# Linear attention and a gated feed-forward on one core: numerators in two column halves in plain float32, normalizers in four column strips

## The chip, the core and the metric

The kernel runs on one core of a Trainium2 chip. Of the core's engines, TensorE (PE in the profile, its weight loads PEld) multiplies matrices into PSUM, VectorE (DVE) and ScalarE (ACT) work element by element, and SyncE (SP) issues the transfers between the chip's memory and SBUF. GpSimd (POOL) does almost nothing here. The metric is the device time in microseconds (us) of one execution; less is better. A head is an attention head; "pair" below means two heads of one batch entry, which the kernel treats together.

## The reference, cut to what matters

```python
# q, k, v: 8 batches x 8 heads x 576 positions x 64; w_phi: 64 x 128
def phi(x):
    proj = einsum('bhsd,df->bhsf', x, w_phi)                     # 128 features
    proj = proj - max(abs(proj), axis=-1, keepdims=True)
    return concatenate([exp(proj), exp(-proj)], axis=-1)         # 256 features
q_p, k_p = phi(q), phi(k)
kv = einsum('bhsf,bhsd->bhfd', k_p, v)                           # 256 x 64 per head
z = sum(k_p, axis=2)                                             # 256 per head
num = einsum('bhsf,bhfd->bhsd', q_p, kv)
den = einsum('bhsf,bhf->bhs', q_p, z)[..., None] + 1e-06
attn = num / den
# x: 4608 tokens x 512; w_gate, w_val: 512 x 1536; w_out: 1536 x 512
out = (1 / (1 + exp(-(x @ w_gate))) * (x @ w_val)) @ w_out
```

`num` is called the numerator and `den` the normalizer below. The two signs of the exponential are two products that accumulate into the same result.

## The kernel before, in words

**Attention.** Positions lie along the free dimension and features along the 128 partitions. For each of the 32 pairs `att_k` projects K (`pk`), takes the maximum of the absolute values, exponentiates (`ek`) and multiplies with V (`kvp`, line 358). V carries a column of ones, so the product has 65 rows: 64 of `kv` and one of `z`. Four small transposes (line 367, `tp`) bring it to 128 features x 65 for each head and sign. `att_q` projects Q (`pq`, lines 397 and 403), and DVE subtracts the maximum, which leaves `d` (line 428, whose instruction is kept in `marks`).

`att_num` runs once for each half of the 576 positions. ACT exponentiates `d` for both signs (`eq`, line 439). For each head the products of line 456 go into one accumulator `nm` of 65 rows: 64 rows of numerators and, as the 65th, the normalizers. ACT copies it to `ex` (line 460). `ps_n` holds a single such accumulator.

**Two number formats.** TensorE multiplies plain float32, or float32r, a float32 rounded to fewer bits, of which the trace writes fp32r on the engines that produce it. From pair 8 on (`WHOLE` = 8) the kernel splits each operand into a rounded part and a residual, and adds three float32r products in place of one float32 product: line 446 rounds the exponentials (`eqh`, ACT), line 447 takes the residual (`eql`, DVE), and `kvh` and `kvl` are the same for the key-value sums. The first eight pairs use plain float32, with `kv` unsplit.

**Normalizing.** `att_norm` gathers the 65th row of `ex` over DMA into 128 partitions x 9 (`dn`, line 469), DVE adds 1e-06 and takes the reciprocal, and two DMAs write it to memory and spread it over 64 partitions (`rb`, lines 472 and 473). `att_scale` multiplies (`xp`, line 484, once for each head) and writes x to memory (`xs`, line 491). Both run for pair i-1 while pair i is worked on.

**Feed-forward.** Five of its 12 blocks of 128 hidden features (`JA` = 5) run beside the attention, in chunks of 256 tokens, as soon as a batch entry's x is there: `gv` (line 136), then the gate on ACT and DVE, then `acc` (line 143). The other seven run after the attention, in chunks of 512 tokens (`g`, `v`, `acc`).

**What sets the order.** The program's order for a pair is: loads, `att_k`, `att_q` of the next pair, `att_norm` of the pair before, the two halves of `att_num`, `att_scale` of the pair before, and one step of loading weights. Between them `fill()` hands out units of feed-forward work. A planner then orders each engine's instructions ahead of time by priority and estimated readiness; attention work has the higher priority (`PRIORITY`), and `issue_after` ties an instruction behind another on its engine. `att_scale` is tied behind the last residual of line 447, or, where there is none, behind the subtraction of line 428. All DMAs are issued by SP in one order. PSUM has eight accumulators of 2 KB a partition: two for `gv`, three for the projections (`ps_p`, tag `pp`), one for `kvp` and `tp`, one for `nm`, one for `acc`.

Of the kernel before, what the change touches and what calls it, by code (L numbers as in the profile page):

```python
# [30 lines left out]
HS = S // 2  # L31
KVW = D + 1

JA = 5  # feed-forward blocks that run beside the attention
JR = 8  # blocks JA to JR - 1 take the attention's bytes, the others phase 1's
WHOLE = 8  # first pairs: plain float32 products, no splits
DIRECT = 4  # first pairs: K's exponentials straight from PSUM
PRIORITY = 400
RATE, LAG = 0.7, 2  # feed-forward units per slot; slots from x to its first unit


@with_exitstack
def attention_moe(
# [20 lines left out]
        for m in marks:  # L64
            stack.enter_context(tc.issue_after(m.ins))

# [1 line left out]
    weights = {}  # L68

    ebias = const.tile([P, 1], F32, name="ebias")  # L70
    vec.memset(ebias, -896.0 * 2.0**23)

    def from_f64(h, l, raw, mid, sp, nb, name):
        # h: the value cut to 12 bits; l: the other bits as an integer times their unit
        words = raw.rearrange("p (n two) -> p n two", two=2)
        lo, hi = words[:, :, 0], words[:, :, 1]
        top = sp.tile([P, DM], U32, tag="wtop", name="wtop" + name, bufs=nb)
        vec.tensor_scalar(top, hi, 0x7FFFFE00, None, op0=ALU.bitwise_and)
        relu = act.activation(top, top, AF.Relu, bias=ebias, scale=8.0)
        vec.scalar_tensor_tensor(  # L80
            top, hi, 0x80000000, top, op0=ALU.bitwise_and, op1=ALU.bitwise_or
        )
        vec.tensor_copy(h, top.bitcast(F32))
        if mid is None:
            rest, unit = hi, lo
            vec.tensor_scalar(
                hi, hi, 16, 0x01FF0000, op0=ALU.logical_shift_left, op1=ALU.bitwise_and
            )
            vec.scalar_tensor_tensor(
                hi, lo, 16, hi, op0=ALU.logical_shift_right, op1=ALU.bitwise_or  # L90
            )
        else:
            words = mid.rearrange("p (n two) -> p n two", two=2)
            rest, unit = words[:, :, 0], words[:, :, 1]
            vec.tensor_scalar(rest, rest, 0x01FFFFFF, None, op0=ALU.bitwise_and)
        vec.tensor_scalar(unit, top, 0xFF800000, None, op0=ALU.bitwise_and)
        return relu, vec.scalar_tensor_tensor(
            l, rest, 2.0**-36, unit.bitcast(F32), op0=ALU.mult, op1=ALU.mult
        )

    def load_weights(j, m, wp, sp, nb, twice):
        if m == 0:
            wh = wp.tile([P, 3 * DM], F32R, tag=f"wh{j}", name=f"wh{j}")
            wl = wp.tile([P, 3 * DM], F32R, tag=f"wl{j}", name=f"wl{j}")
            weights[j] = (wh, wl)
        wh, wl = weights[j]
        ms = slice(m * DM, m * DM + DM)
        raw = sp.tile([P, 2 * DM], U32, tag="wraw", name=f"wraw{j}_{m}", bufs=nb + 1)
        load, mid = nc.sync.dma_start(raw, w_moe[j, :, m, :].bitcast(U32)), None
        if twice:  # L110
            # the same rows two bytes on: a word then holds the bits below h's
            mid = sp.tile([P, 2 * DM], U32, tag="wmid", name=f"wmid{j}_{m}", bufs=nb)
            nc.sync.dma_start(
                mid[:, : 2 * DM - 1].bitcast(U16),
                w_moe[j, :, m, :].bitcast(U16)[:, 1 : 4 * DM - 1],
            )
        return load, *from_f64(wh[:, ms], wl[:, ms], raw, mid, sp, nb, f"{j}_{m}")
# [135 lines left out]
            xs = nxt  # L253
        out_step(*late)

# [1 line left out]
    with ExitStack() as actx:  # L257
        wp1 = actx.enter_context(tc.tile_pool(name="wp1", bufs=1))
        moe = actx.enter_context(tc.tile_pool(name="moe1", bufs=2))
        at1 = actx.enter_context(tc.tile_pool(name="at1", bufs=1, side="right"))  # L260
        at = actx.enter_context(tc.tile_pool(name="at", bufs=2, side="right"))
        ps_gv = actx.enter_context(tc.tile_pool(name="ps_gv", bufs=2, space=PSUM))
        ps_p = actx.enter_context(tc.tile_pool(name="ps_p", bufs=3, space=PSUM))
        ps_kv = actx.enter_context(tc.tile_pool(name="ps_kv", bufs=1, space=PSUM))
        ps_n = actx.enter_context(tc.tile_pool(name="ps_n", bufs=1, space=PSUM))
        ps_acc = actx.enter_context(tc.tile_pool(name="ps_o", bufs=1, space=PSUM))

        ident = at1.tile([KVW, KVW], F32, name="ident")
# [24 lines left out]
        def att_k(b, p):  # L293
# [71 lines left out]
            tp = ps_kv.tile([P, 4, KVW], F32, tag="kvp", name="tp" + n)  # L365
            for i in range(4):
                nc.tensor.transpose(tp[:, i, :], kvt[:, i, :], ident)
            if b * NP + p < WHOLE:
                kv = at.tile([P, 4, KVW], F32, tag="kv", name="kv" + n)
                act.copy(kv, tp)  # L370
                kvs[b, p] = (kv,)
            else:
                kvh = at.tile([P, 4, KVW], F32R, tag="kv", name="kvh" + n)
                kvl = at.tile([P, 4, KVW], F32R, tag="kvl", name="kvl" + n)
                split(kvh, kvl, tp)
                kvs[b, p] = (kvh, kvl)

        def att_q(b, p):
            n = f"{b}_{p}"
# [46 lines left out]
                pm.unsqueeze(2).broadcast_to([P, nj, 32]),  # L426
            )
            marks.append(vec.tensor_tensor(d, d, mb, op=ALU.subtract))
            ex = at.tile([KVW, 2, S], F32, tag="ex", name="ex" + n)
            qst[b, p] = (d, ex)  # L430

        def att_num(b, p, hf):
            n = f"{b}_{p}_{hf}"
            d, ex = qst[b, p]
            cs = slice(hf * HS, hf * HS + HS)
            terms = []
            for sg in range(2):
                e = at.tile([P, 2, HS], F32, tag="eq", name=f"eq{n}_{sg}", bufs=2)
                act.activation(e, d[:, :, cs], AF.Exp, scale=1.0 - 2.0 * sg)
                if len(kvs[b, p]) == 1:  # L440
                    terms.append([(kvs[b, p][0], e)])
                else:
                    kvh, kvl = kvs[b, p]
                    eh = at.tile([P, 2, HS], F32R, tag="eqh", name=f"eqh{n}_{sg}", bufs=2)
                    el = at.tile([P, 2, HS], F32R, tag="eql", name=f"eql{n}_{sg}", bufs=2)
                    act.copy(eh, e)
                    late[b, p, hf, sg] = vec.tensor_tensor(
                        el, e, eh.bitcast(F32), op=ALU.subtract
                    )
                    terms.append([(kvh, eh), (kvl, eh), (kvh, el)])  # L450
            for hd in range(2):
                nm = ps_n.tile([KVW, HS], F32, tag="nm", name=f"nm{n}_{hd}")
                last = len(terms[0]) - 1
                for sg in range(2):
                    for i, (a, x) in enumerate(terms[sg]):
                        nc.tensor.matmul(  # L456
                            nm, a[:, 2 * hd + sg, :], x[:, hd, :],
                            start=sg == 0 and i == 0, stop=sg == 1 and i == last,
                        )
                act.copy(ex[:, hd, cs], nm)  # L460

        def att_norm(b, p):
            n = f"{b}_{p}"
            _, ex = qst.pop((b, p))
            dn = at.tile([P, 9], F32, tag="dn", name="dn" + n)
            rb = at.tile([D, 2, S], F32, tag="rb", name="rb" + n, bufs=1)
            scr = dens[b * NP + p]
            for hd in range(2):
                nc.sync.dma_start(dn[hd * D : hd * D + D, :], ex[D : D + 1, hd, :])
            vec.tensor_scalar(dn, dn, 1e-6, None, op0=ALU.add)  # L470
            vec.reciprocal(dn, dn)
            nc.sync.dma_start(scr.rearrange("h (r c) -> (h r) c", c=9), dn)
            nc.sync.dma_start(
                rb.rearrange("p h s -> p (h s)"),
                scr.rearrange("h s -> (h s)").unsqueeze(0).broadcast_to([D, 2 * S]),
            )
            rbs[b, p] = (ex, rb)

        def att_scale(b, p):
            n = f"{b}_{p}"  # L480
            ex, rb = rbs.pop((b, p))
            xp = at.tile([P, S], F32, tag="xp", name="xp" + n, bufs=2)
            for hd in range(2):
                vec.tensor_tensor(
                    xp[hd * D : hd * D + D, :], ex[0:D, hd, :], rb[:, hd, :], op=ALU.mult
                )
            t = 0
            while t < S:
                c, o = divmod(b * S + t, CH)
                w = min(CH - o, S - t)  # L490
                nc.sync.dma_start(
                    xscr[c][:, p * CH + o : p * CH + o + w], xp[:, t : t + w]
                )
                t += w
# [31 lines left out]
        for i, (b, p) in enumerate(steps):  # L526
# [9 lines left out]
            if i:  # L536
                attend(att_norm, *steps[i - 1])
            fill()
            attend(att_num, b, p, 0)
            fill()  # L540
            attend(att_num, b, p, 1)
            if i:
                m = late.get((b, p, 1, 1), marks[-1])
                with tc.issue_after(m.ins):
                    attend(att_scale, *steps[i - 1])
            while wdone < min(3 * JA, 4 * i + 1):
                with tc.issue_after(marks[-1].ins):
# [90 lines left out]
```

## Time and profile before

| | |
|---|---|
| Median of the runs | 1304.68 us (1303.23 to 1305.15, 3 runs) |
| Profiled execution, first to last instruction | 1307.2 us |
| Mean granted TensorE clock | 0.992 |
| TensorE busy | 1269.8 us, 97% |
| VectorE busy | 877.5 us, 67% |
| ScalarE busy | 650.7 us, 50% |
| Numerators of line 456, first to last start | 23.8 to 686.7 us |

The span is that of one profiled execution, and its length is taken as this execution's own time; it lies 2.5 us above the median. Engine rows in a timeline give start and length in microseconds, engine, line, operation, the tile written and the tiles read, and partitions x elements. A group row gives a line's instructions together: how many, busy time, mean nanoseconds of one, then the idle time of the engine just before them and what ended it. "128*65" after a product means 128 rows and 65 columns of the array in use. A busy TensorE can hold overlapping products, so starts say more than lengths.

### The profile page before, as it was taken

To read this page: it belongs to the slowest core of one execution; us is meant where nothing else is said; L and a number is where in the kernel's file an instruction comes from. 1 tells how busy PE (TensorE), PEld (TensorE's weight loads), DVE (VectorE), ACT (ScalarE), POOL (GpSimd) and SP (SyncE) were. 2 spreads that over 40 slices of the span, in tenths; PEclk is the share of its full clock that TensorE was granted. 3 is DMA by queue.
4 is the path that set the end of the run, shared out by engine and by line. 5 is a ranking of instruction groups with operands and counts; after the bars stand their busy time and mean duration, and the time that the engine had idled before them with its cause. 6 is when DMAs were issued, how large, how long until landed. Compare 5 with 4: busy or idle time off the path is not lost.

```text
span 1307.2 us, 19107 instructions
## 1 busy us (share of the span) xinstructions
PE 1269.8 (97%) x7112; PEld 1070.8 (82%) x7112; DVE 877.5 (67%) x1778; ACT 650.7 (50%) x1416; POOL 0.6 (0%) x6
## 2 busy tenths in 40 slices
PE   7878999999999999999999999999999999999998
PEld 4545788999898989898998988888888888888886
DVE  5777989899899888989866958834343443434333
ACT  5754777777777787777754523322222222222221
POOL 0000000000000000000000000000000000000000
PEclk9988999999999999999999999999999999999999
DMA  5576543233233323332225424313021211202010
GB/s 190 165 216 195 167 131 100 85 107 105 86 115 86 107 84 118 94 108 76 61 69 180 130 78 132 97 65 97 1 97 33 65 50 48 97 1 97 1 65 33
DMA packets 75166, 125.12 MB, mean 96 GB/s; under 512 B 18496, under 2 KB 38080, under 8 KB 75072
## 3 DMA queue, kind: packets, MB, share of 16 engines
q1 hardware_dynamic: 75072, 123.89, 30.7%
q8 instruction: 56, 0.92, 0.3%
q14 instruction: 38, 0.31, 0.1%
HBM read 95.25 MB, written 28.46 MB: 95 GB/s over the span
## 4 chain that ended last, share of the span: by engine, by line
PE 88%; DVE 4%; DMA 4%; ACT 2%; issue 1%; SPq 0%; DVEq 0%; ACTq 0%
PE acc L143 22%; PE gv L136 17%; PE g L136 13%; PE v L136 13%; PE kvp L358 9%; PE nm L456 7%; PE pk L316 3%; PE pq L403 2%; PE pq L397 1%; DMA xs<-xp 1%; DMA q<-q 1%; DMA rb<-den 1%; DMA dn<-ex 1%; ACT ek L338 1%; DMA wraw<-w_moe 1%
## 5 line engine op out<-in xcount | busy, mean ns | idle before, releaser
L136 PE MATMUL gv<-xh,wh 128*128 128x256 f32 x720 | 208.3, 290 | 3.6 <-DVE t L156 3.4
L136 PE MATMUL gv<-xh,wl 128*128 128x256 f32 x720 | 206.5, 287 | 0.0
L136 PE MATMUL gv<-xl,wh 128*128 128x256 f32 x720 | 206.2, 286 | 0.0
L60 ACT CAST hh<-u 128x256 fp32r<-128x256 f32 (+1 forms) x153 | 75.4, 494 | 245.3 <-DVE u L157 245.1
L143 PE MATMUL acc<-wh,hh 128*128 128x512 f32 x432 | 171.3, 397 | 0.7 <-ACT y L187 0.7
L143 PE MATMUL acc<-wl,hh 128*128 128x512 f32 x432 | 169.9, 393 | 0.0
L143 PE MATMUL acc<-wh,hl 128*128 128x512 f32 x432 | 166.1, 394 | 0.1
L358 PE MATMUL kvp<-ek,v 128*65 128x256 f32 x640 | 158.6, 383 | 6.9 <-ACT ek L338 5.3
L155 DVE TENSOR_SCALAR t<-t 128x256 uint32<-128x256 uint32 (+1 forms) x153 | 52.5, 344 | 154.6 <-ACT t L152 153.7
L136 PEld LDWEIGHTS gv<-xh,wh 128*128 128x128 f32 x720 | 137.1, 191 | 10.0 <-DVE t L156 4.7
L136 PEld LDWEIGHTS gv<-xl,wh 128*128 128x128 f32 x720 | 137.0, 190 | 3.3
L136 PEld LDWEIGHTS gv<-xh,wl 128*128 128x128 f32 x720 | 137.0, 190 | 2.3
L358 PEld LDWEIGHTS kvp<-ek,v 128*65 128x65 f32 x640 | 86.6, 138 | 49.4 <-ACT ek L338 9.7
L61 DVE TENSOR_TENSOR hl<-u,hh 128x256 fp32r<-128x256 f32 (+1 forms) x153 | 81.1, 531 | 47.2 <-ACT hh L60 46.1
L152 ACT ACTIVATE t<-g 128x512 f32<-128x512 f32 x63 | 37.6, 597 | 150.0 <-PE g L136 149.8
L156 DVE SCALAR_TENSOR_TENSOR t<-t,v 128x512 f32<-128x512 f32 x63 | 43.3, 687 | 85.6 <-PE v L136 85.4
L136 PE MATMUL g<-xh,wh 128*128 128x512 f32 x252 | 99.0, 393 | 0.0
L136 PE MATMUL v<-xh,wh 128*128 128x512 f32 x252 | 98.6, 391 | 0.0
L136 PE MATMUL g<-xl,wh 128*128 128x512 f32 x252 | 98.6, 391 | 0.0
L136 PE MATMUL g<-xh,wl 128*128 128x512 f32 x252 | 98.5, 391 | 0.0
L136 PE MATMUL v<-xl,wh 128*128 128x512 f32 x252 | 98.3, 390 | 0.0
L136 PE MATMUL v<-xh,wl 128*128 128x512 f32 x252 | 98.2, 390 | 0.0
(91 smaller groups left out, 2533.6 us busy)
## 6 DMA issues: line engine op xcount, KB each, us to landing
wraw<-w_moe SPq DMA_DIRECT2D x36, 512.0 KB, 3.9
xl<-xs SPq DMA_DIRECT2D x36, 512.0 KB, 4.1
v<-v SPq DMA_DIRECT2D x32, 325.0 KB, 3.3
k<-k SPq DMA_DIRECT2D x32, 320.0 KB, 3.1
q<-q SPq DMA_DIRECT2D x32, 288.0 KB, 3.2
rb<-den SPq DMA_DIRECT2D x32, 288.0 KB, 3.8
ys<-y SPq DMA_DIRECT2D x36, 256.0 KB, 2.1
yp<-ys SPq DMA_DIRECT2D x36, 256.0 KB, 4.3
```

The costliest lines, as they stand in the source:

```text
L60: a = act.copy(h, x)
L61: return a, vec.tensor_tensor(l, x, h.bitcast(F32), op=ALU.subtract)
L136: nc.tensor.matmul(o, a[:, ws], x[:, cs], start=i == 0, stop=i == 11)
L143: nc.tensor.matmul(acc, a[:, ts], w[:, ws], start=first and i == 0, stop=last and i == 2)
L152: act.activation(t, g, AF.Tanh, scale=0.5)
L155: vec.tensor_scalar(tu, tu, 0x7FFFFFFF, None, op0=ALU.bitwise_and)
L156: vec.scalar_tensor_tensor(t, t, 1.0, vl, op0=ALU.add, op1=ALU.mult)
L316: nc.tensor.matmul(o, x[:, ts], w, start=t == 0, stop=t == len(terms) - 1)
L338: act.activation(e[:, i, sg * F : sg * F + F], pp[:, i, :], AF.Exp, bias=(mn, mx)[sg][:, i : i + 1], scale=1.0 - 2.0 * sg,)
L358: nc.tensor.matmul(kvp[:, hd, :], vx[:, slot, :], es[t // 2][:, slot % 4 if t < 4 else 0, :], start=t == 0, stop=t == 4,)
L403: nc.tensor.matmul(pp, wq[:, i, 2 * F :], s[:, hd, cs], start=i == 0, stop=i == 1,)
L456: nc.tensor.matmul(nm, a[:, 2 * hd + sg, :], x[:, hd, :], start=sg == 0 and i == 0, stop=sg == 1 and i == last,)
```

## The change

The splits of the key-value sums and of Q's exponentials go, for all pairs. `kv` is plain float32, 64 columns, and the sums `z` go into a tile of their own, `zs`, each repeated over 32 columns. Q's exponentials are taken for the whole 576 positions at once, one tile for each sign. The numerators of head 0 are written to partitions 0 to 63 and those of head 1 to partitions 64 to 127 of one accumulator `nm`, so each product uses 64 of the array's 128 columns. The normalizers are products of their own, with 32 equal columns, one strip of 32 columns for each head and half, all into one accumulator `dp`, which takes a buffer of the projections. `ps_p` goes from three buffers to two and `ps_n` from one to two. `ex` now has both heads on 128 partitions, so `xp` is one multiplication; gathering the normalizers takes four DMAs in place of two, and spreading the reciprocals two in place of one. `att_scale` is tied to the subtraction of line 428 alone. Comments are dropped.

```diff
-        ps_p = actx.enter_context(tc.tile_pool(name="ps_p", bufs=3, space=PSUM))
+        ps_p = actx.enter_context(tc.tile_pool(name="ps_p", bufs=2, space=PSUM))
-        ps_n = actx.enter_context(tc.tile_pool(name="ps_n", bufs=1, space=PSUM))
+        ps_n = actx.enter_context(tc.tile_pool(name="ps_n", bufs=2, space=PSUM))
...
-            if b * NP + p < WHOLE:
-                kv = at.tile([P, 4, KVW], F32, tag="kv", name="kv" + n)
-                act.copy(kv, tp)
-                kvs[b, p] = (kv,)
-            else:
-                kvh = at.tile([P, 4, KVW], F32R, tag="kv", name="kvh" + n)
-                kvl = at.tile([P, 4, KVW], F32R, tag="kvl", name="kvl" + n)
-                split(kvh, kvl, tp)
-                kvs[b, p] = (kvh, kvl)
+            kv = at.tile([P, 4, D], F32, tag="kv", name="kv" + n)
+            act.copy(kv, tp[:, :, 0:D])
+            zs = at.tile([P, 4, 32], F32, tag="zs", name="zs" + n)
+            vec.tensor_copy(zs, tp[:, :, D : D + 1].broadcast_to([P, 4, 32]))
+            kvs[b, p] = (kv, zs)
...
+        def att_num(b, p):
+            n = f"{b}_{p}"
+            d = qst.pop((b, p))
+            kv, zs = kvs.pop((b, p))
+            es = []
             for sg in range(2):
+                e = at.tile([P, 2, S], F32, tag=f"eq{sg}", name=f"eq{n}_{sg}", bufs=1)
+                act.activation(e, d, AF.Exp, scale=1.0 - 2.0 * sg)
+                es.append(e)
+
+            ex = at.tile([P, S], F32, tag="ex", name="ex" + n)
+            for hf in range(2):
+                cs = slice(hf * HS, hf * HS + HS)
+                nm = ps_n.tile([P, HS], F32, tag="nm", name=f"nm{n}_{hf}")
                 for sg in range(2):
+                    for hd in range(2):
                         nc.tensor.matmul(
+                            nm[hd * D : hd * D + D, :], kv[:, 2 * hd + sg, :],
+                            es[sg][:, hd, cs], start=sg == 0, stop=sg == 1,
                         )
+                act.copy(ex[:, cs], nm)
+
+            dp = ps_p.tile([P, HS], F32, tag="pp", name=f"dp{n}")
+            for sg in range(2):
+                for hd in range(2):
+                    for hf in range(2):
+                        o = 32 * (2 * hd + hf)
+                        nc.tensor.matmul(
+                            dp[o : o + 32, :], zs[:, 2 * hd + sg, :],
+                            es[sg][:, hd, hf * HS : hf * HS + HS],
+                            start=sg == 0, stop=sg == 1, tile_position=(0, o),
+                        )
+            dr = at.tile([P, HS], F32, tag="dr", name="dr" + n, bufs=1)
+            late[b, p] = act.copy(dr, dp)
+            rbs[b, p] = (ex, dr)
...
-            for hd in range(2):
-                nc.sync.dma_start(dn[hd * D : hd * D + D, :], ex[D : D + 1, hd, :])
+            for g in range(4):
+                nc.sync.dma_start(
+                    dn[g * 32 : g * 32 + 32, :], dr[32 * g : 32 * g + 1, :]
+                )
...
-            for hd in range(2):
-                vec.tensor_tensor(
-                    xp[hd * D : hd * D + D, :], ex[0:D, hd, :], rb[:, hd, :], op=ALU.mult
-                )
+            vec.tensor_tensor(xp, ex, rb, op=ALU.mult)
...
             if i:
-                m = late.get((b, p, 1, 1), marks[-1])
-                with tc.issue_after(m.ins):
+                with tc.issue_after(marks[-1].ins):
                     attend(att_scale, *steps[i - 1])
```

More of the change, by code (lines that the diff above doesn't have):

```diff
@@ L428, in att_q @@
             marks.append(vec.tensor_tensor(d, d, mb, op=ALU.subtract))
[L429 to L436, printed above, removed]
-            for sg in range(2):
[L438 to L448, printed above, removed]
-                    )
-                    terms.append([(kvh, eh), (kvl, eh), (kvh, el)])
-            for hd in range(2):
-                nm = ps_n.tile([KVW, HS], F32, tag="nm", name=f"nm{n}_{hd}")
-                last = len(terms[0]) - 1
@@ new lines, in att_q @@
+            qst[b, p] = d
+        def att_num(b, p):
[3 more added lines that the diff above has]
+            es = []
+            for sg in range(2):
+                e = at.tile([P, 2, S], F32, tag=f"eq{sg}", name=f"eq{n}_{sg}", bufs=1)
[5 more added lines that the diff above has]
+                nm = ps_n.tile([P, HS], F32, tag="nm", name=f"nm{n}_{hf}")
@@ L454, in att_num @@
                 for sg in range(2):
-                    for i, (a, x) in enumerate(terms[sg]):
+                    for hd in range(2):
                         nc.tensor.matmul(
-                            nm, a[:, 2 * hd + sg, :], x[:, hd, :],
-                            start=sg == 0 and i == 0, stop=sg == 1 and i == last,
-                        )
-                act.copy(ex[:, hd, cs], nm)
+                            nm[hd * D : hd * D + D, :], kv[:, 2 * hd + sg, :],
+                            es[sg][:, hd, cs], start=sg == 0, stop=sg == 1,
+                        )
@@ L462, in att_norm @@
+            dr = at.tile([P, HS], F32, tag="dr", name="dr" + n, bufs=1)
+            late[b, p] = act.copy(dr, dp)
+            rbs[b, p] = (ex, dr)
         def att_norm(b, p):
             n = f"{b}_{p}"
-            _, ex = qst.pop((b, p))
+            ex, dr = rbs.pop((b, p))
             dn = at.tile([P, 9], F32, tag="dn", name="dn" + n)
-            rb = at.tile([D, 2, S], F32, tag="rb", name="rb" + n, bufs=1)
+            rb = at.tile([P, S], F32, tag="rb", name="rb" + n, bufs=1)
             scr = dens[b * NP + p]
-            for hd in range(2):
-                nc.sync.dma_start(dn[hd * D : hd * D + D, :], ex[D : D + 1, hd, :])
+            for g in range(4):
+                nc.sync.dma_start(
+                    dn[g * 32 : g * 32 + 32, :], dr[32 * g : 32 * g + 1, :]
+                )
@@ L472, in att_norm @@
             nc.sync.dma_start(scr.rearrange("h (r c) -> (h r) c", c=9), dn)
[L473 to L476, printed above, removed]
+            for hd in range(2):
+                nc.sync.dma_start(
+                    rb[hd * D : hd * D + D, :],
+                    scr[hd].unsqueeze(0).broadcast_to([D, S]),
+                )
             rbs[b, p] = (ex, rb)
@@ L482, in att_scale @@
             xp = at.tile([P, S], F32, tag="xp", name="xp" + n, bufs=2)
-            for hd in range(2):
-                vec.tensor_tensor(
-                    xp[hd * D : hd * D + D, :], ex[0:D, hd, :], rb[:, hd, :], op=ALU.mult
-                )
+            vec.tensor_tensor(xp, ex, rb, op=ALU.mult)
             t = 0
@@ L538, in attention_moe @@
             fill()
-            attend(att_num, b, p, 0)
+            attend(att_num, b, p)
             fill()
-            attend(att_num, b, p, 1)
             if i:
-                m = late.get((b, p, 1, 1), marks[-1])
-                with tc.issue_after(m.ins):
+                with tc.issue_after(marks[-1].ins):
                     attend(att_scale, *steps[i - 1])
```

## The prediction

> **What bounds the kernel now.** I read the page's first two parts, then the busy time of the engines by stretches of 100 us, because the kernel has stages with different limits.
>
> ```profile
> span 1307.2 us, 19107 instructions
> PE 1269.8 (97%) x7112; PEld 1070.8 (82%) x7112; DVE 877.5 (67%) x1778; ACT 650.7 (50%) x1416; POOL 0.6 (0%) x6
> ```
>
> ```profile
> 0.00:100.00 100.00, 79.07 (x318) 49.45 (x319) 69.61 (x165) 62.42 (x168) 0.60 (x6) 0.95 0.59 188
> 100.00:200.00 100.00, 92.19 (x557) 73.86 (x556) 87.79 (x187) 65.03 (x146) 0.00 (x0) 0.97 0.53 160
> ...
> 300.00:400.00 100.00, 100.00 (x690) 89.88 (x689) 90.18 (x189) 74.16 (x168) 0.00 (x0) 1.00 0.32 95
> ...
> 600.00:700.00 100.00, 99.84 (x696) 91.20 (x695) 74.45 (x163) 61.17 (x143) 0.00 (x0) 1.00 0.23 65
> ```
>
> The columns are the stretch, then busy microseconds of PE, PEld, DVE, ACT and POOL, the granted clock, the DMA share and GB/s. From 200 us on TensorE has no gap: 100.00 of 100. In the first 200 us it is idle for 200 - 79.07 - 92.19 = 28.7 us. A busy TensorE could still be a waiting one, since the ends of matmuls are modelled. So I looked at starts in the timeline of TensorE, in the middle of that stage.
>
> ```profile
> 412.15 0.28 PE L136 MATMUL gv<-xl,wh 128*128 128x256 f32 x1
> 412.27 0.29 PE L456 MATMUL nm<-eqh,kvh 128*65 128x288 f32 x1
> 412.40 0.29 PE L456 MATMUL nm<-eqh,kvl 128*65 128x288 f32 x1
> 412.53 0.29 PE L456 MATMUL nm<-eql,kvh 128*65 128x288 f32 x1
> 412.66 0.29 PE L456 MATMUL nm<-eqh,kvh 128*65 128x288 f32 x1
> 412.79 0.29 PE L456 MATMUL nm<-eqh,kvl 128*65 128x288 f32 x1
> 412.92 0.29 PE L456 MATMUL nm<-eql,kvh 128*65 128x288 f32 x1
> 413.06 0.28 PE L136 MATMUL gv<-xh,wl 128*128 128x256 f32 x1
> ```
>
> Starts, not durations, are the price. Six rounded products of a numerator start within 413.06 - 412.27 = 0.79 us, **0.132 us each**, and feed-forward products follow without a gap. So in this stage the kernel is TensorE's instruction stream laid end to end, and a microsecond added to it or taken from it is a microsecond of the time. DVE at 90 of 100 and ACT at 74 are close behind, but nothing in the stream waits for them.
>
> **The numerators before.** A late pair (pairs 8 to 31) has two halves, two heads, two signs and three terms, 24 products. 24 x 0.132 = **3.16 us**. An early pair (0 to 7) has eight plain float32 products. Each stands in the trace as two passes, as the counts of line 456 show:
>
> ```profile
> L456 PE MATMUL nm<-eqh,kvh x192: 288/293/485, 175.3 to 686.5; 128*65 128x288 f32 x192
> ...
> L456 PEld LDWEIGHTS nm<-eq,kv x128: 133/138/234, 23.8 to 167.7; 128*65 128x65 f32 x128
> L456 PE MATMUL nm<-eq,kv x128: 403/406/687, 23.8 to 168.0; 128*65 128x288 f32 x128
> its engine sat idle before it (us, times) until:
> ACT ex L460: 8.3, 13
> ACT kv L370: 7.3, 12
> ```
>
> ```profile
> 140.23 1.13 PE L456 MATMUL nm<-eq,kv 128*65 128x288 f32 x4
> ```
>
> 128 passes over 8 pairs are 16 for a pair, and four of them end 1.13 us after the first began, so the step is (1.13 - 0.406) / 3 = **0.241 us**, which I call a slot. An early pair costs 16 x 0.241 = **3.86 us**. The late rows run from 175.3 to 686.5 us, 511 us for 24 pairs, 21.3 us a pair.
>
> **The numerators and normalizers after.** Every pair has eight float32 products of 64 columns (16 passes) and eight of 32 columns (16 passes), all streaming 288 columns: 32 passes. Nothing in this trace runs two products side by side in the array, so the price is bounded from both sides. If the passes run one after another: 32 x 0.241 = 7.71 us. If two heads run beside each other in the two halves, and four normalizers in the four strips: 16/2 + 16/4 = 12 slots, 2.89 us. I take 12 slots: each consecutive product in the new code addresses other columns and another accumulator, and the steps above show that TensorE already starts a product long before the one before it has ended (0.29 us long, 0.132 us apart).
>
> To that comes the **turn** of the array from full width to halves, to strips, and back. Below, its bound is nothing: a pass of 65 columns and a full one alternate at the plain step in the rows from 412.15 on. Above, a pass that can neither be fed nor loaded ahead shows its tail and its load, 0.406 - 0.241 + 0.138 = 0.30 us. The nearest row is the small transposes between feed-forward products:
>
> ```profile
> 405.46 0.41 PE L367 MATMUL tp<-ident,kvt 65*128 65x65 f32 x4
> 405.68 0.36 PE L136 MATMUL gv<-xh,wh 128*128 128x256 f32 x1
> 405.88 0.28 PE L136 MATMUL gv<-xl,wh 128*128 128x256 f32 x1
> 405.99 0.28 PE L136 MATMUL gv<-xh,wl 128*128 128x256 f32 x1
> ```
>
> The first full product after them is followed at 0.20 us instead of the 0.12 of the next step: 0.08 us lost where only the shape changed. A turn also changes how the array is divided, so I take 0.15 us, half of the upper bound. I count six turns a pair: the exponentials of sign 1 come one activation later than those of sign 0, so I expect two runs, each halves, then strips, then full width. 12 x 0.241 + 6 x 0.15 = **3.79 us** a pair. The Trainium skill, in "TensorEngine Tiling (Array Packing)", section "Key Properties", says that changing the tiling mode drains TensorE, which speaks against this change; the transposes' 0.08 us stays within one mode, so no run here shows the rule yet. In "TensorE: Matmul & The Clock Gate", section "Measured speedup vs the span model", three column tiles gave 2.38 times; at that share of the ideal (0.79) the 12 slots would be an estimated 15.2, and the sum below about 25 us higher.
>
> Late pairs: 3.79 - 3.16 = +0.63 us, x24 = +15.1. Early pairs: 3.79 - 3.86 = -0.07, x8 = -0.6. Sum **+14.5 us**, or 192 turns x 0.15 = 28.8, less 14.3 gained by the slots.
>
> **The other engines.** These rows give what leaves and what comes:
>
> ```profile
> L439 ACT ACTIVATE eq<-d 128x576 f32<-128x576 f32 x128 | 86.3, 689 | 12.2 <-DVE eql L447 7.3 <-PE nm L456 4.7
> L447 DVE TENSOR_TENSOR eql<-eq,eqh 128x576 fp32r<-128x576 f32 x96 | 70.2, 752 | 11.0 <-ACT eqh L446 9.6 <-PE pq L403 1.2
> L446 ACT CAST eqh<-eq 128x576 fp32r<-128x576 f32 x96 | 60.7, 671 | 37.7 <-PE nm L456 37.7
> L460 ACT COPY ex<-nm 65x288 f32<-65x288 f32 x128 | 50.1, 392 | 22.1 <-PE nm L456 20.8 <-DMA den<-dn 1.0
> L484 DVE TENSOR_TENSOR xp<-ex,rb 64x576 f32<-64x576 f32 x64 | 47.9, 749 | 10.9 <-DMA rb<-den 10.4
> L61 DVE TENSOR_TENSOR kvl<-tp,kvh 128x260 fp32r<-128x260 f32 x24 | 10.2, 423 | 11.2 <-ACT kvh L60 11.1
> ```
>
> A late pair loses on DVE four residuals (4 x 0.752), the residual of the key-value sums (0.42) and one of two multiplications (0.75), and gains a copy of 128 columns (at most 0.42): 3.8 us less of 21.3. ACT loses four casts (4 x 0.671) and one of four evictions (0.39); its exponentials become two of 1152 columns for four of 576: some 3.1 us less. Since TensorE waits for neither in the stage without gaps, I price all of it at nothing. What covers them is TensorE's own stream; if that cover went, the relief would be a gain, not a cost.
>
> The multiplication by the reciprocals moves: it was queued on DVE behind the last residual, and is now behind the subtraction of Q's maximum only. If the reciprocals aren't back, the gating of the feed-forward waits behind it on DVE, and TensorE for a free accumulator. Below that costs nothing. Above, the whole way of the normalizers, from these rows 1.8 + 1.7 + 3.8 = 7.3 us, would stand on DVE: 90% of 21.3, less 3.8, plus 7.3 is 22.7 us, 1.4 us over the period and 34 us in all.
>
> ```profile
> rb<-den SPq DMA_DIRECT2D x32, 288.0 KB, 3.8
> dn<-ex SPq DMA_DIRECT2D x64, 2.2 KB, 1.8
> den<-dn SPq DMA_DIRECT2D x32, 4.5 KB, 1.7
> ```
>
> I take nothing: L484 waited 10.9 us over 64 times, and the normalizers start a whole pair earlier. Each pair issues three more DMAs on SP (four instead of two to gather the normalizers, two instead of one to spread the reciprocals). SP holds the loads of Q, K, V, weights and x behind them; those come a pair ahead, so this too costs nothing, or 3.8 us once at the last pair, which has no next one to hide in. The second numerator buffer can take at most the 8.3 us that TensorE waited for the one being emptied (L460), all in early pairs; the third projection buffer that it replaces can cost as much there, as eight tiles a pair now share two buffers. I let these two cancel and keep 8 us either way for the range.
>
> The sum is made against the profiled execution: 1307.2 + 14.5 = 1321.7. Its span lies 2.5 us above the median, 1304.7, so the forecast for the median is **1319 us**.
>
> **Rivals.** (1) The turn is hidden, on the other side of no change: if the next weights are loaded while the last pass drains, a turn costs under 0.075 us (14.3 / 192), and the 12 slots decide. At no cost: late -0.27 x 24, early -0.97 x 8, **1290 us**. For it: the steps from 412.15 on hide every load. Against it: the 0.08 us behind the transposes. (2) Order limits the packing: the two passes of one product use the same columns, and if a waiting pass holds up those behind it, a run of eight passes (a a b b a a b b) takes five slots instead of four or two. Two runs of numerators and two of strips are 20 slots, 4.83 us, with turns 5.73: +2.57 x 24 = 61.7, and +1.87 x 8 = 15, half of it in the idle 28.7 us: **1374 us**; without turns 1349. For it: passes of one product always follow each other directly in the trace; against it: nothing there shows a pass held up by columns. By the same Clock Gate page, section "The mechanism", matmuls stay in program order, which is what this rival needs. (3) Nothing runs side by side and the change packs nothing: 32 slots. (7.71 - 3.16) x 24 + (7.71 - 3.86) x 8 = 109 + 31, **1445 us**. For it: float32 takes 0.241 us where the rounded type takes 0.132, so streaming may be what is short, and two streams need twice as much; against it: the rounded type already streams the same bytes nearly twice as fast.
>
> **Numbers.** The forecast has 0.40, with its own range from turns of 0.08 to 0.30 us: 1305 to 1347. Rival 1 has 0.22, rival 2 0.22, rival 3 0.16. The range is 1286 to 1400: it holds all but rival 3, and 1286 allows 4 us of the early waits gone beside rival 1. A measurement of this kernel tells about 0.2%, 2.6 us, from no change. Faster: 0.19 of rival 1 and 0.04 of the forecast, 0.23. Within: 0.03 and 0.08, 0.11. Slower: the remaining 0.28 and both other rivals, 0.66.
>
> **What would show it.** In the timeline of TensorE, the starts of the numerator passes: two in each 0.24 us (packed), eight in five times 0.24 us (rival 2), or one in each 0.24 us (rival 3); for the normalizers four, again eight in five, or one. The step from the last strip to the next feed-forward product shows the turn. TensorE must stay at 100 of 100 from 200 us on; DVE should fall by 3.8 / 21.3, to some 72 of 100. The forecast is wrong if DVE or ACT shows in TensorE's waits there, or if the planner scatters the runs so that turns are many more than six a pair.

## The result, and the profile after

The changed kernel takes 1373.44 us (median; 1372.13 to 1377.45), the kernel before in the same comparison 1304.91 us. The ratio is 1.0528, 95% interval 1.0509 to 1.0547: **slower by 68.5 us**, where 14.5 us slower was forecast. The page of the changed kernel and its busy time by stretches (stretch, busy PE, PEld, DVE, ACT and POOL, granted clock, DMA share, GB/s):

```profile
span 1370.9 us, 19378 instructions
PE 1294.5 (94%) x7432; PEld 1036.1 (76%) x7432; DVE 800.7 (58%) x1658; ACT 588.6 (43%) x1224; POOL 0.6 (0%) x6
```

```profile
0.00:100.00 100.00, 65.99 (x312) 39.32 (x312) 59.20 (x143) 50.23 (x130) 0.60 (x6) 0.89 0.54 172
100.00:200.00 100.00, 87.20 (x539) 65.07 (x542) 71.71 (x167) 51.60 (x110) 0.00 (x0) 0.92 0.45 142
...
300.00:400.00 100.00, 96.26 (x677) 75.40 (x676) 68.72 (x154) 58.68 (x127) 0.00 (x0) 1.00 0.29 90
...
700.00:800.00 100.00, 88.92 (x622) 74.37 (x621) 61.78 (x143) 42.43 (x92) 0.00 (x0) 0.97 0.29 92
```

TensorE now has gaps in every stretch of the attention: 79.07 of the first 100 us became 65.99, and the stretch from 300 to 400 us, which had none, shows 96.26. TensorE's waits in the overlapped stage, of which the kernel before had none longer than 1.4 us, begin with these (waiting line, releaser: total, times, longest; from 136 to 760 us):

```profile
PE pk L321 <- DVE dk L344: 2.5, 1, 2.5
PE gv L136 <- ACT xh L60: 2.1, 2, 1.1
```

DVE fell as worked out (from 90.18 to 68.72 of 100; 72 was forecast, and part of the fall is that the pairs are further apart), and the time did not fall with it.

The new products themselves do what the change says. Timeline of TensorE in the changed kernel:

```profile
417.26 0.28 PE L136 MATMUL gv<-xh,wh 128*128 128x256 f32 x1
417.38 0.28 PE L136 MATMUL gv<-xl,wh 128*128 128x256 f32 x1
417.59 2.16 PE L443 MATMUL nm<-eq,kv 128*64 128x288 f32 x16
419.68 1.17 PE L454 MATMUL dp<-eq,zs 128*32 128x288 f32 x14
420.78 0.38 PE L316 MATMUL pk<-wq,kh 128*128 128x256 f32 x1
421.09 0.67 PE L454 MATMUL dp<-eq,zs 128*32 128x288 f32 x2
421.70 0.39 PE L316 MATMUL pk<-wq,kh 128*128 128x256 f32 x1
```

Sixteen passes of numerators take 2.16 us, of which 0.406 is the last pass's own length: 1.75 us for the seven slots before it, 0.25 us a slot with two passes in each. So two heads run side by side at nearly the full rate.

**Where the 64 us between the two spans lie.** For each kind of product I multiplied the number of passes in the trace by the step at which it follows its like without a wait (0.241 us for a full float32 pass of 288 columns, half of it in column halves, a quarter in strips, 0.131 for a rounded one, and so on), and set the sum against the time up to TensorE's last product. What remains is the time in which TensorE turned, was not fed, or made its steps more slowly.

| us | before | after | difference |
|---|---|---|---|
| K, Q and feed-forward products | 1142.5 | 1142.5 | 0 |
| numerators and normalizers at their steps | 106.3 | 92.7 | -13.6 |
| remainder up to the first feed-forward product | 40.1 | 70.7 | +30.6 |
| remainder from there to the last numerator | 9.5 | 43.8 | +34.3 |
| remainder after it | 3.0 | 16.0 | +13.0 |

The slots gave 13.6 us, where 14.3 were forecast. The remainder grew by 78 us. Of these, 39 are gaps in which TensorE stood still (1307.2 - 1269.8 = 37.4 us before, 1370.9 - 1294.5 = 76.4 after), and some 15 are turns, at the price measured below. The other 24 were not taken apart; the granted clock, 0.982 over the span in place of 0.992, is a candidate. The first feed-forward product came 19.7 us later, as line 136 shows in the two kernels, before first and after second (first and last start behind the durations):

```profile
L136 PE MATMUL gv<-xh,wh x720: 274/283/579, 116.2 to 774.0; 128*128 128x256 f32 x180
```

```profile
L136 PE MATMUL gv<-xh,wh x720: 274/283/582, 135.9 to 838.4; 128*128 128x256 f32 x180
```

### The profile page after: what moved, and what is told of

It reads as the page before. It is cut to its first block, busy times and chain, and to the rows that moved or that the text cites. A ratio compares the mean times of both kernels' runs of the same rounds, so it can differ in the third digit from the quotient of the medians.

```text
span 1370.9 us, 19378 instructions
## 1 busy us (share of the span) xinstructions
PE 1294.5 (94%) x7432; PEld 1036.1 (76%) x7432; DVE 800.7 (58%) x1658; ACT 588.6 (43%) x1224; POOL 0.6 (0%) x6
## 4 chain that ended last, share of the span: by engine, by line
PE 78%; DVE 11%; DMA 5%; ACT 2%; issue 2%; SPq 1%; DVEq 0%; ACTq 0%
PE acc L143 19%; PE gv L136 15%; PE g L136 13%; PE v L136 13%; PE kvp L358 8%; PE nm L443 3%; DMA wmid<-w_moe 3%; PE pk L316 2%; PE dp L454 2%; PE pq L399 2%; DVE d L424 1%; DVE mb L420 1%; DMA xl<-xs 1%; DVE pm L409 1%; DVE wl L97 1%
## 5 line engine op out<-in xcount | busy, mean ns | idle before, releaser
L358 PE MATMUL kvp<-ek,v 128*65 128x256 f32 x640 | 164.5, 399 | 18.8 <-ACT ek L338 16.2
L358 PEld LDWEIGHTS kvp<-ek,v 128*65 128x65 f32 x640 | 89.5, 144 | 67.4 <-ACT ek L338 21.4
L143 PEld LDWEIGHTS acc<-wh,hh 128*128 128x128 f32 x432 | 81.3, 188 | 19.8 <-ACT y L187 3.9
```

The lines of the kernel that those rows point to most:

```text
L143: nc.tensor.matmul(acc, a[:, ts], w[:, ws], start=first and i == 0, stop=last and i == 2)
L358: nc.tensor.matmul(kvp[:, hd, :], vx[:, slot, :], es[t // 2][:, slot % 4 if t < 4 else 0, :], start=t == 0, stop=t == 4,)
```

## The experiments

The first suspicion was the exchange of buffers. **Theory B**: the third projection buffer, given away, is the loss. **Theory O**: the new form itself is.

**Three projection buffers again, in the changed kernel.**

```diff
-  ps_p = actx.enter_context(tc.tile_pool(name="ps_p", bufs=2, space=PSUM))
+  ps_p = actx.enter_context(tc.tile_pool(name="ps_p", bufs=3, space=PSUM))
-  ps_n = actx.enter_context(tc.tile_pool(name="ps_n", bufs=2, space=PSUM))
+  ps_n = actx.enter_context(tc.tile_pool(name="ps_n", bufs=1, space=PSUM))
```

> The changed kernel with the buffers as before: three for the projections (and the normalizers' accumulator among them), one for the numerators. Theory B (the loss is the third projection buffer that the change gives away): most of the 68.5 us comes back, 1300 to 1315 us, TensorE idle before the first feed-forward product falls from some 46 us of 136 to near the 21 us of 100 before, and pk and pq follow without waits. Theory O (the loss is in the numerators' new form: whole-length exponentials, packed runs, the normalizers' way): the time stays at 1350 or more.

Measured: 1363.21 us, ratio 1.0447 (1.0417 to 1.0477). 56.6 us over the kernel before in place of 68.5: only 12 us came back. Theory B, as put, falls.

**Two projection buffers in the kernel before**, nothing else.

```diff
-  ps_p = actx.enter_context(tc.tile_pool(name="ps_p", bufs=3, space=PSUM))
+  ps_p = actx.enter_context(tc.tile_pool(name="ps_p", bufs=2, space=PSUM))
-  ps_n = actx.enter_context(tc.tile_pool(name="ps_n", bufs=1, space=PSUM))
+  ps_n = actx.enter_context(tc.tile_pool(name="ps_n", bufs=2, space=PSUM))
```

> The kernel before, with nothing changed but the buffers: two for the projections, two for the numerators. Theory B: most of the loss appears without any of the new products, 1345 to 1375 us, with waits at pk and pq. Theory O: 1300 to 1310 us, no change.

Measured: 1321.18 us, ratio 1.0111 (1.0094 to 1.0128), 15 us slower, between the two theories. The third buffer has a price, but a fifth of the loss.

**The normalizers' accumulator out of the projections' ring**, with two and two buffers as changed.

```diff
-            dp = ps_p.tile([P, HS], F32, tag="pp", name=f"dp{n}")
+            dp = ps_n.tile([P, HS], F32, tag="nm", name=f"dp{n}")
```

> The changed kernel with the normalizers' accumulator taken from the numerators' two buffers in place of the projections' two. It tells whether, under theory B, the eighth tile in the projections' ring matters or the ring's being two. If the eighth tile: 1310 to 1335 us. If two buffers are short for the seven projection tiles alone: 1350 to 1375 us. Theory O: unchanged at 1365 to 1380 us.

Measured: 1324.78 us, ratio 1.0142 (1.0121 to 1.0162). 18 us over the kernel before: one line brings back 50 of the 68.5 us. That rules out theory O for the greater part, and with the first run it says that neither the number of buffers nor the products matter most, but *which ring* the normalizers' accumulator stands in.

**Theory C.** Buffers of a ring are handed out in the program's order: K of pair i, Q of pair i+1, the normalizers `dp` of pair i, K of pair i+1. In a ring of two, the second K tile of pair i+1 reuses the buffer of `dp` of pair i. So it waits until pair i's K has been projected, exponentiated, multiplied with V and transposed, the sums have been multiplied with Q's exponentials, and the normalizers have been copied out (`dr`, line 460). Before, K's tiles followed Q's alone, and ran ahead. The trace shows both. Timelines of TensorE and ACT: first the kernel before, where these are K's first product of pair 20 and the last eviction of pair 19's numerators; then the changed kernel from one `dr` to the next:

```profile
409.18 0.28 PE L316 MATMUL pk<-wq,kh 128*128 128x256 f32 x1
...
435.87 0.39 ACT L460 COPY ex<-nm 65x288 f32<-65x288 f32 x1
```

```profile
399.14 0.40 ACT L460 COPY dr<-dp 128x288 f32<-128x288 f32 x1
...
400.51 0.39 PE L316 MATMUL pk<-wq,kh 128*128 128x256 f32 x2
...
405.26 0.46 PE L321 MATMUL pk<-wk,k 128*128 128x128 f32 x2 [0.21 <-PE acc L143]
...
408.71 2.75 PE L358 MATMUL kvp<-ek,v 128*65 128x256 f32 x12
...
411.50 0.58 ACT L364 COPY kvt<-kvp 65x512 f32<-65x512 f32 x1 [0.27 <-PE kvp L358]
...
414.90 0.37 ACT L369 COPY kv<-tp 128x256 f32<-128x256 f32 x1 [2.52 <-PE tp L367]
...
417.59 2.16 PE L443 MATMUL nm<-eq,kv 128*64 128x288 f32 x16
419.68 1.17 PE L454 MATMUL dp<-eq,zs 128*32 128x288 f32 x14
...
421.80 0.40 ACT L460 COPY dr<-dp 128x288 f32<-128x288 f32 x1 [0.15 <-PE dp L454]
```

Before, K of pair 20 starts 27 us ahead of pair 19's end, more than a whole pair (21.3 us); over the 31 pairs it is 13.3 to 32.3 us. In the changed kernel the second K tile starts 0.1 to 3.4 us *after* the eviction, in every pair. The pair's links are then one closed loop. Their means over pairs 8 to 30: `dr` to K's second tile 2.0, to its third 1.8, to the end of `kvp` 8.6, to the end of `kv` 3.6, to the numerators 2.5, to the next `dr` 4.5, together 23.0 us. That sum is the distance of the pairs by construction, since each link begins where the one before ended; what shows that the loop is closed is its first link, which is never below zero. With three buffers (the first run) K's third tile is held in place of the second: it starts 0.7 to 3.5 us after the eviction, and the pairs are 23.2 us apart. With `dp` in the numerators' ring K's second tile starts 9.8 us before the eviction, and the loop is open.

The list of TensorE's waits hardly names `dr` (`pk` waited 2.1 us for it, four times in all): this fits the planner, which orders TensorE ahead of time and can put the second tile late in that order. In the first pairs, with no feed-forward product to put into the waits, TensorE stood still (44 us before the first feed-forward product, in place of 25); later the planner filled most of them.

**Theory D**, its rival: the packed form stretches the pairs by itself. Against it stand the distances of the same pairs, from last eviction to last eviction: 21.8 us in the kernel before, 21.9 with `dp` in the numerators' ring, and 19.2 in the best packed form below.

**The same loop closed in the kernel before**, with no packed product:

```diff
-                nm = ps_n.tile([KVW, HS], F32, tag="nm", name=f"nm{n}_{hd}")
+                if hf and hd:
+                    nm = ps_p.tile([KVW, HS], F32, tag="pp", name=f"nm{n}_{hd}")
+                else:
+                    nm = ps_n.tile([KVW, HS], F32, tag="nm", name=f"nm{n}_{hd}")
```

> The kernel before, all buffers as they were, but the last of a pair's four numerator accumulators is taken from the projections' ring of three. No packed product, no longer exponentials. Theory C: the next pair's K projections now wait for this pair's numerators, 1340 to 1365 us. Theory D: 1303 to 1312 us.

Measured: 1445.63 us, ratio 1.1069 (1.1052 to 1.1085), far above what theory C had put down. The stage that had no gaps, and the longest of TensorE's waits from 200 to 800 us (total, times, longest):

```profile
300.00:400.00 100.00, 91.82 (x579) 78.14 (x580) 74.32 (x156) 63.79 (x143) 0.00 (x0) 0.95 0.28 81
400.00:500.00 100.00, 87.78 (x573) 75.70 (x572) 75.95 (x152) 62.65 (x140) 0.00 (x0) 0.95 0.28 83
```

```profile
PE nm L459 <- DVE kvl L61: 15.8, 10, 2.8
```

The numerators' wait for the residual of the key-value sums, which the kernel before did not show in that stretch, now comes first: the rounding steps lie in the loop, which may be why it is longer than the changed kernel's (the pairs are 26.3 us apart). K's third tile, which started 21.8 us ahead of the last eviction of the pair before, now starts 0.7 us behind it on average. The loop's length was not taken apart.

One accumulator of each pair in the wrong ring costs 140 us without anything else of the change. Theory D cannot account for that.

**The loop opened by the program's order**, with `dp` in the projections' ring and two and two buffers, as changed; `att_den` holds the normalizers' products and the copy `dr`, and stands behind the next pair's K and Q:

```diff
             if i:
+                attend(att_den, *steps[i - 1])
                 attend(att_norm, *steps[i - 1])
```

> The changed kernel, buffers as changed (two and two, normalizers' accumulator in the projections' ring), but the normalizers' products of a pair are written behind the next pair's K and Q projections in the program. Theory C: the K projections come before it in the ring and no longer wait for the chain, 1320 to 1335 us. Theory D, or if an eighth tile in a ring of two is the cost by its number alone: 1360 to 1380 us.

Measured: 1339.33 us, ratio 1.0253 (1.0229 to 1.0278): 35 us back, a little less than expected. K's second tile starts 8 to 23 us ahead of `dr` here. The direction is theory C's. What is left over may be the price of an eighth tile in a ring of two, which this run does not separate from the rest.

**`dp` in a buffer of its own** (two for projections, one for numerators, one for `dp`):

```diff
...
-            dp = ps_p.tile([P, HS], F32, tag="pp", name=f"dp{n}")
+            dp = ps_d.tile([P, HS], F32, tag="dp", name=f"dp{n}")
```

> The changed kernel with two buffers for projections, one for numerators and one for the normalizers alone. Theory C: the projections are free of the chain, 1320 to 1335 us (15 us of it for the ring of two, as the kernel before showed). Theory D: 1345 or more.

Measured: 1330.32 us, ratio 1.0191 (1.017 to 1.0213), as theory C had it.

**`dp` in the numerators' ring, buffers as in the kernel before** (three and one):

```diff
...
-            dp = ps_p.tile([P, HS], F32, tag="pp", name=f"dp{n}")
+            dp = ps_n.tile([P, HS], F32, tag="nm", name=f"dp{n}")
```

> The changed kernel with the buffers as in the kernel before (three for projections, one for numerators), and the normalizers' accumulator in the numerators' ring. Theory C (what costs is that the normalizers' accumulator stands in the projections' ring, so that the next pair's K projections wait until this pair's whole chain has reached the normalizers): 1308 to 1320 us, from before 1306.6, less 13.6 for the slots, plus some 20 for 61 runs of narrow products at 0.35 us of turning in and out, plus what the shared numerator buffer costs. Theory D (the packed form itself stretches the pairs): 1325 or more, as with two buffers and the accumulator moved.

Measured: 1333.63 us, ratio 1.0231 (1.0196 to 1.0267). A miss, and in the range that the expectation gave to theory D. With a single accumulator the planner broke the numerators into runs of one half each, 99 runs of narrow products in place of the 61 on which the expectation rested. The price of a run can be read where it stands between two feed-forward products, as here in the run with `dp` in the numerators' ring:

```profile
316.52 0.28 PE L136 MATMUL gv<-xh,wh 128*128 128x256 f32 x1
316.73 2.16 PE L443 MATMUL nm<-eq,kv 128*64 128x288 f32 x16
318.82 0.39 PE L136 MATMUL gv<-xl,wh 128*128 128x256 f32 x1
```

From the start of the one feed-forward product to the start of the other a run of 8 numerator passes takes 1.33 us, of 16 passes 2.30, of 16 strip passes 1.32. Less 0.12 for the feed-forward product's own step and the slots (0.96, 1.93, 0.96) each leaves 0.23 to 0.25 us for **turning in and out**; numerators and strips in one run leave 0.40. The expectation had 0.35. So 99 runs cost 24.8 us where some 20 were expected, and the larger part of the miss of 14 to 26 us is not explained by them. What a single accumulator costs beyond the turns was not taken apart; the next run shows that the packed form is not it.

**Three projection buffers, used by nothing else, and whole runs**: the second half's numerators in the key-value sums' ring, the first half's and `dp` in the numerators'.

```diff
-        ps_p = actx.enter_context(tc.tile_pool(name="ps_p", bufs=2, space=PSUM))
+        ps_p = actx.enter_context(tc.tile_pool(name="ps_p", bufs=3, space=PSUM))
...
-        ps_n = actx.enter_context(tc.tile_pool(name="ps_n", bufs=2, space=PSUM))
+        ps_n = actx.enter_context(tc.tile_pool(name="ps_n", bufs=1, space=PSUM))
...
-                nm = ps_n.tile([P, HS], F32, tag="nm", name=f"nm{n}_{hf}")
+                if hf:
+                    nm = ps_kv.tile([P, HS], F32, tag="kvp", name=f"nm{n}_{hf}")
+                else:
+                    nm = ps_n.tile([P, HS], F32, tag="nm", name=f"nm{n}_{hf}")
...
-            dp = ps_p.tile([P, HS], F32, tag="pp", name=f"dp{n}")
+            dp = ps_n.tile([P, HS], F32, tag="nm", name=f"dp{n}")
```

> The changed kernel with three buffers for the projections, none of them used by anything else: the first half's numerators and the normalizers use the one numerator buffer, the second half's the buffer of the key-value sums. If the loss was the place in the projections' ring, the loss of the third buffer and the turns, and nothing else, then 1306 less 13.6 for the slots plus 32 pairs x 0.5 to 0.7 us of turns = 1308 to 1315 us, the best of the packed forms, and no packed form beats the kernel before. If the key-value ring now holds up the next pair in the projections' place: 1330 or more. Under 1303 would mean that the relief of VectorE and ScalarE is worth something after all.

Measured: 1318.42 us, ratio 1.009 (1.0071 to 1.0109), the best packed form, and 3 us over the expected range. 67 runs, seven of them of both kinds (0.40 us) and 60 of one (0.25), are 17.8 us of turns. Its remainder is 76.8 us, so 59.0 lie outside the turns, against 52.6 in the kernel before. The products of the change therefore cost 17.8 - 13.6 = 4.2 us here; 11.2 was measured, and some 6 to 7 us stay open. A gain from the relief of DVE and ACT does not show.

**The packing's order.** Signs innermost, so that four passes for the same columns follow each other before the other head's come:

```diff
-                for sg in range(2):
-                    for hd in range(2):
+                for hd in range(2):
+                    for sg in range(2):
                         nc.tensor.matmul(
                             nm[hd * D : hd * D + D, :], kv[:, 2 * hd + sg, :],
...
-            for sg in range(2):
-                for hd in range(2):
-                    for hf in range(2):
+            for hd in range(2):
+                for hf in range(2):
+                    for sg in range(2):
                         o = 32 * (2 * hd + hf)
```

> The changed kernel with the products of one column group issued one after another (signs innermost: four passes on the same columns, then four on the next) in place of alternating groups. If a pass that waits for its columns holds up those behind it, a half takes 7 slots in place of 4 and the strips 13 in place of 4, that is 15 slots or 3.6 us more a pair: about 1373 + 32 x 3.6 = 1490 us at most, 1440 or more with some of it in TensorE's idle time. If passes for other columns get past a waiting one, 1365 to 1385 us, as the changed kernel.

Measured: 1396.6 us, ratio 1.0693 (1.0674 to 1.0712). Neither number. But the products answer the question that it was made for:

```profile
448.38 2.21 PE L443 MATMUL nm<-eq,kv 128*64 128x288 f32 x16
450.52 1.20 PE L454 MATMUL dp<-eq,zs 128*32 128x288 f32 x16
```

2.21 us where 14 slots would be 3.5: a pass that waits for its columns does not hold up passes for other columns, at least four deep. The trace does not name the columns of a pass, so this rests on the program's order having been kept; that the first two passes start 14 ns apart here, and 7 ns in the changed kernel, fits it. The 22 us over the changed kernel (90.0 over the kernel before in place of 68.5) are not in these rows. The loop is 24.0 us there in place of 23.0, spread over the links from `kvp` on; why is left open.

**Packed numerators for the first eight pairs alone**, rounded ones after that, buffers as before. The packed exponentials are taken in halves, which share the buffers of the rounded kernel's exponentials (`eq` and `eqh`).

```diff
+            if b * NP + p < WHOLE:
+                if hf == 0:
+                    att_num_packed(b, p)
+                return
```

> A mixture: pairs 0 to 7, which used plain float32 before, get the packed numerators and the normalizers in strips (accumulators over the numerator and the key-value rings, none in the projections'), pairs 8 to 31 stay with the three rounded products of the kernel before; buffers as before. Their slots cost 2.89 us and their turns 0.5 to 0.7 in place of 3.86, so at most 0.3 to 0.5 us a pair is gained, 2.5 to 4 us where TensorE sets the pace, and the first pairs, which wait for copies of a single accumulator four times a pair, may gain some more: 1297 to 1306 us, the version that could beat both. If turns and the key-value ring cost as much in the first pairs as they save: 1305 to 1312.

Measured: 1321.78 us, ratio 1.0115 (1.0097 to 1.0133), 1.2% slower than the kernel before and outside both of the expected ranges. TensorE stood at 33.90 of 40 us from 160 to 200 us, where the two forms meet, against 38.30 before; whether the shared SBUF buffers or the key-value ring hold it there was not told apart. None of the versions run beats the kernel before.

## Why the prediction was wrong

**What bounds the kernel**: right. TensorE's stream end to end is the time, and gaps in it lengthen the kernel. "From 200 us on TensorE has no gap" is a little too strong: the prediction's own row from 600 to 700 us has 99.84, and the next one of the kernel before, which holds the end of the overlap, is lower still:

```profile
700.00:800.00 100.00, 97.26 (x618) 86.81 (x617) 76.86 (x181) 42.52 (x90) 0.00 (x0) 1.00 0.43 140
```

**The price of the products**: right in kind, too high in size. Twelve slots were forecast and twelve are there. A turn was priced at 0.15 us and is 0.12 to 0.13 (0.25 for in and out, 0.40 for the three of a run of both kinds). Six turns a pair, 192 in all, were counted; the changed kernel has 44 runs, 28 of them of both kinds, which makes 116 turns and 15.2 us in place of 28.8. So its products cost some 15.2 - 13.6 = 1.6 us and not 14.5. That the best packed form is 11.2 us slower, near the forecast, is chance: its turns and slots account for 4.2 of them. The rule quoted from the Trainium skill, "TensorEngine Tiling (Array Packing)", section "Key Properties", that a change of mode drains TensorE, agrees with the 0.25 us a run. The measured 2.38 times for three strips, quoted from the Trainium skill, "TensorE: Matmul & The Clock Gate", section "Measured speedup vs the span model", is a lower share than this case shows. In the changed kernel 16 strip passes take 1.18 us:

```profile
397.90 1.18 PE L454 MATMUL dp<-eq,zs 128*32 128x288 f32 x16
```

Three further slots of four strip passes take 1.18 - 0.406 = 0.77 us, 0.26 a slot against 0.241 for a single pass, 3.7 times in four strips.

**The step that failed** is the one on the buffers: "the third projection buffer that it replaces can cost as much there, as eight tiles a pair now share two buffers. I let these two cancel and keep 8 us either way". It counted the tiles of the ring and priced their number. That exchange of buffers alone costs 15 us net (the kernel before with two and two), so the two did not cancel even there. It didn't ask, for the new eighth tile, when it comes free and who stands behind it. `dp` comes free at the end of the longest chain of the pair, and the next pair's K stands behind it. Moving it alone gave 50 us. The 18 us that were left with it moved are near the sum of the exchange of buffers, 15, and of turns less slots, 2. The prediction asked that question of DVE's order and SP's queue, not of the ring.

**The multiplication moved on DVE**, bounded at 34 us and taken as nothing, and the **three DMAs**: no run isolated them. After the last numerators TensorE waits once for 6.1 us for the feed-forward's x (`xh`), where 3.8 were allowed for the last pair; with `dp` in the numerators' ring, and the same DMAs, no wait for `xh` is longer than 1.4. The best packed form has both, and they may have a part in the 6 to 7 us that stay open there.

**The rivals.** Rival 2 gave 1374 us, the measured time, and is wrong all the same: it needs passes held up by those in front of them, and 16 passes run in 2.16 us, not in 10 slots. The agreement is chance; only the rows of the products told the two causes apart. Rival 3 falls by the same rows. Rival 1 falls by the turns of 0.12 to 0.13 us: its break-even was 0.075. The list lacked the case that came true, a new wait where the kernel before had none.

**The signs named in advance** did their work: "TensorE must stay at 100 of 100 from 200 us on" failed at 96.26, and the rows above name DVE and ACT in TensorE's waits, as "the forecast is wrong if" had said. As a sign the second is weak: the kernel before waits for DVE and ACT there too, at most 1.4 us at a time; what changed is how long.

## What to carry to other kernels

A ring of accumulators is a queue in the program's order. Before a new tile is put into one, write down who takes the buffer next, and what that one used to run ahead of: if the new tile ends a chain and the next user starts one, the chains of successive rounds are closed into a loop, and one more buffer need not open it (here it gave back 12 of 68.5 us). When a forecast's number comes out by another mechanism, look at the rows that the mechanism must show before believing it.

Narrow float32 products in separate columns packed at nearly the full factor here (0.25 us for two passes and 0.26 for four, against 0.241 for one), but paid 0.25 us for each run between full-width products. Write them so that a run is long, and count the runs that the planner makes, not the products.

## What the runs showed of the hardware that I had not expected

Four passes for one column group queued in a row did not hold back the passes for the next group (2.21 us in place of 2.16 for 16 passes): they wait by columns, not in one line, as far as four deep, if the program's order was kept. And the granted clock can fall where TensorE waits: with the loop closed in the kernel before it was 0.95 from 300 to 400 us, with TensorE busy for 91.82 of 100, in place of 1.00. At 96.26 of 100, in the changed kernel, it stayed at 1.00. So a gap may cost more than its length; no run measured by how much.
